# Operand blocks of the feed-forward: other units, a fourth staging tile, and two operands split in the first period

## The chip, the core and the metric

The kernel runs on one core of one Trainium2 chip. The metric is the device time of one execution in microseconds (us), the median of three runs. The core has five engines that work beside each other, each in the order of its own instruction list: PE multiplies matrices, DVE, ACT and POOL work on elements, and SP only issues transfers (ACT issues some too). An instruction that waits holds back everything behind it on its engine. SBUF holds operands, PSUM holds what PE writes, DRAM holds inputs, outputs and what the kernel parks there.

## The reference

One transformer block over 2048 tokens of width 576 in float32, with a conditioning vector `c`:

```python
mod = (_silu(c) @ w_mod).reshape(c.shape[0], 6, 1, -1)
sa, ca, ga, sb, cb, gb = ...                      # six rows of 576
h = _layernorm(x) * (1 + ca) + sa
x = x + ga * attention(h, wq, wk, wv, wo, beta)   # 32 heads of 18, four segments of 512 tokens
h = _layernorm(x) * (1 + cb) + sb
x = x + gb * ((_silu(h @ w_gate) * (h @ w_up)) @ w_down)   # inner width 4608
```

Attention runs inside each segment of 512 tokens under a causal mask and is mixed, by a gate per head, with a linear memory that collects the earlier segments.

## The kernel before

The kernel has three stretches: projections and memory (to about 260 us), attention (to about 632 us), and the feed-forward with the output projection of the last segment at its head.

**Attention** is a loop over 33 units `u` (L1332); a unit is four heads of one segment, so segment `s` is units 8s to 8s+7. A unit has eleven steps `k`. Which small piece of work stands in which step is written out by hand in `PAT`, a table of letters: `M` and `X` are the output projection of an earlier segment, `V` the probabilities times values, `n` the hand-over of row maxima through DRAM (ACT stores them, SP reads them back as `qs<-mD`), and so on. At the start of unit u SP also issues the keys and queries of unit u+3. Besides the table there is a dictionary `sched`, filled by `at(g, f)`, where `g = 11*u + k`: what stands under g is issued at the end of that step.

**The feed-forward** multiplies by seven products instead of eight: tokens come in two halves, features in two halves of 288, and seven combinations of the four blocks (operands 0 to 6 of `y`) meet seven combinations of the weights (`O`). A float32 operand is split into a high part (a cast on ACT) and the rest (a subtraction on DVE); each product is then three products of parts, seven matmuls in all, the last being for the remaining 32 features, held three times over 96 rows. Each block of features is thus three pieces `kb`: 128, 128 and 96 rows.

The operands of the first 1024 tokens are made during attention, by `stage_a` and `stage_b`, which put their work into `sched`:

- `stage_a` takes the first 512 tokens. For six blocks `i` (two feature halves `kh` times three `kb`) it loads the normalized columns from DRAM (`load_cols`, L931, shown as `yh<-xh`), transposes them on PE (`trans4`, `pt`, L947), scales and shifts them on ACT into `yh` (L942), and then, in two column halves, casts (L926), subtracts (L909) and stores the split to DRAM (`yD`, L915 and L917) as operands 0 and 1. The two parts go through a staging tile; three of them are used in turn, one in a free part of `yh` and two in `mbd`, the memory of attention, which is no longer read. Block `i` belongs to unit 18 + i; its transposes stand in the step that `step_of` (table `KP`, L46) gives, its cast two steps later for the first half and five for the second, the subtraction one step after the cast, the store two more.
- `stage_b` takes the other 512 tokens in the same way, block `i` in unit 24 + i. It forms the differences with the first blocks on POOL (L1005) and stores operand 5; the blocks for the others stay in `yh`, nine pieces of 512 columns (`yh[:, k]`, k = 0 to 2).

**The border** begins after the last unit (L1352). SP loads the first weight block `O` (`load_o`, L1114), then operands 0, 1 and 5 (`load_y`, L1103), with the second weight block between operand 0 and 1. POOL forms operand 4 (`y_sum` 0 to 2, L1017) and operand 6 (`y_sum` 3 to 5, L1019) and the sums of the weight blocks (`sum_o`, L1139, four for each block). PE does the output projection of the last segment: 32 pieces `n`, four to a half of 288 columns (`wo_m`, `pw`, L709), into two PSUM banks in turn; after a half DVE adds it to x (`wo_x`, `xr`, L714), which frees the bank. Between the pieces stand, at the numbers in the tables, a weight sum (`SS`, L48), the split of one piece of an operand that stays in SBUF (`HH`, L49, `y_here`, cast L1026, subtractions L1028 and L1030), and the split of weights (`WW`, L47: `prep_w`, `wh` L1148 and `wl` L1149; `prep_r` for the remaining 32 features, `wr` L1133 and L1134). `y_here(j)` is operand 4, 3, 6, 2 for j = 0-2, 3-5, 6-8, 9-11. DVE's part of a split is put on a list and issued after the next piece (`flush`).

**Periods.** Then come 2 x 18 periods `p` of fourteen steps (L1440). A step issues what the step before put on the list, casts the weights needed five products later, and then one product (`step`, `prod`, L1184). In period 0 the products of the first half use operands 0, 4, 1, 5, 3, 6 in steps 0 and 2 to 6 and operand 2 in step 8 (`ZM`, L898; `ACT_OP`, L900). Products collect in the PSUM banks A, B and C; ACT copies partial results out of A (`cu`, `tb`, `tc`, L1213) and DVE finishes others (L1199 to L1208). After the first copy ACT issues the stores of both summed weight blocks (`store_o`, `oD<-O`, L1123, L1486). The next weight block is loaded into the buffer of the first once that is stored and its splits are done. In period 0 POOL also scales and sums the down-projection weights (`dr_`, L1162, L1167). From period 1 on, a generator `prep2` (L1032) makes the operands of the other 1024 tokens a step at a time; its pool `x2p` is opened before period 0.

## Time and profile before

| what | value |
|---|---|
| median of three runs | 1934.17 us (1931.89 to 1936.68) |
| the profiled execution's own time | 1936.01 us |
| its span, first to last instruction | 1934.3 us, at a mean clock of 0.993 |
| PE busy | 1879.5 us, 97% of the span |
| DVE, ACT, POOL busy | 1508.3, 934.0, 578.6 us |
| units 18 to 31 | about 461 to 632 us |
| the border, until the first feed-forward product | about 632 to 663.7 us |

The chain that ended last is followed back from the last instruction, at each step to what released it. A timeline line reads: start, duration, engine, line of the kernel, operation, output and inputs, shapes and count; the square brackets hold the idle time of that engine just before, and what ended it. A window line gives, for a stretch of time, its length and then the busy time of PE, PE's weight loads, DVE, ACT and POOL, with the number of instructions, then the clock that PE was granted, the busy share of the transfer engines and GB/s.

### The profile page before, as it was taken

The numbers are of one execution on the slowest core, as the hardware profiler recorded it, in microseconds if no ns is written. First come the engines' busy times: TensorE is split into PE (matmuls) and PEld (weight loads), VectorE is DVE, ScalarE is ACT, GpSimd is POOL, SyncE is SP. The second block draws the span as 40 slices with busy tenths as digits, with TensorE's granted clock in tenths as the row PEclk, the third lists the DMA queues.
The fourth block names the chain that finished last, engine by engine and source line by source line (L and its number), as shares of the span: only waits on it lengthen the run. The fifth ranks groups of instructions, "written<-read, shape, count | busy, mean of one in ns | idle before, by whom it ended". The sixth has DMA issues, their size and how long they took to land.

```text
span 1934.3 us, 30685 instructions
## 1 busy us (share of the span) xinstructions
PE 1879.5 (97%) x10927; PEld 1564.6 (81%) x10927; DVE 1508.3 (78%) x3270; ACT 934.0 (48%) x2057; POOL 578.6 (30%) x778
## 2 busy tenths in 40 slices
PE   7999999999999799999999999999999999999999
PEld 4888865676666678888888888888888888888888
DVE  6475257878776688888888988876888888888887
ACT  2222256767667444445445444444545444454542
POOL 5222235455455464544553544410000000000000
PEclk9999999999999899999999999999999999999999
DMA  7767565445753755455455454468333233332331
GB/s 214 236 228 247 200 201 142 131 139 161 186 146 102 237 181 199 148 184 176 148 174 170 156 168 154 137 232 280 100 96 107 94 122 101 121 101 92 107 109 61
DMA packets 178409, 304.12 MB, mean 157 GB/s; under 512 B 25648, under 2 KB 105968, under 8 KB 176400
## 3 DMA queue, kind: packets, MB, share of 16 engines
q1 hardware_dynamic: 148144, 244.56, 40.7%
q10 hardware_dynamic: 30112, 57.60, 8.5%
q8 instruction: 86, 1.41, 0.3%
q14 instruction: 67, 0.55, 0.1%
HBM read 189.02 MB, written 113.05 MB: 156 GB/s over the span
## 4 chain that ended last, share of the span: by engine, by line
PE 85%; DMA 6%; DVE 4%; ACT 1%; issue 1%; POOL 1%; SPq 1%; DVEq 0%; POOLq 0%; ACTq 0%
PE A L1184 23%; PE pd L1305 12%; PE C L1184 11%; PE pd L1288 9%; PE B L1184 6%; PE pp L98 4%; PE s L586 4%; PE av L606 3%; PE s L184 3%; PE pv L98 3%; PE pw L709 2%; DMA y<-yD 2%; DMA mD<-mr 1%; PE pn L780 1%; DMA wml<-in_w_mod_dram 1%
## 5 line engine op out<-in xcount | busy, mean ns | idle before, releaser
L1184 PE MATMUL A<-y,wh 128*128 128x512 f32 x1152 | 406.8, 394 | 2.9 <-DMA y<-yD 1.5
L189 DVE CUSTOM_DVE_ANT_0 junk<-s,tri 128x256 bf16<-128x256 f32 (+3 forms) x512 | 228.8, 486 | 79.2 <-PE s L184 70.0
L1149 DVE TENSOR_TENSOR wl<-O,wh 128x256 fp32r<-128x256 f32 x504 | 264.5, 530 | 3.6 <-ACT wh L1148 3.1
L1184 PEld LDWEIGHTS A<-y,wh 128*128 128x128 f32 x1152 | 217.1, 188 | 47.6 <-issue 1.7
L1184 PE MATMUL A<-y,wl 128*128 128x512 f32 x576 | 227.2, 394 | 0.0
L589 ACT ACTIVATE Pt<-s 128x512 f32<-128x512 f32 (+1 forms) x352 | 187.1, 559 | 81.8 <-PE s L586 64.8
L1139 POOL TENSOR_TENSOR O<-O 128x384 f32<-128x384 f32 x144 | 162.3, 1139 | 186.6 <-DMA O<-in_wgu_dram 81.3
L1293 DVE TENSOR_TENSOR acc<-acc,pd 128x576 f32<-128x576 f32 x216 | 162.5, 752 | 58.6 <-PE pd L1288 51.8
L1184 PE MATMUL C<-y,wh 128*128 128x512 f32 x576 | 202.8, 393 | 3.8 <-DVE cu L1207 3.8
L1148 ACT CAST wh<-O 128x256 fp32r<-128x256 f32 x504 | 196.7, 405 | 2.0 <-DVE wr L1134 1.0
L1305 PE MATMUL pd<-dh,ah 128*128 128x288 f32 x640 | 189.2, 296 | 0.1
L1305 PE MATMUL pd<-dh,al 128*128 128x288 f32 x640 | 189.1, 295 | 0.0
L1305 PE MATMUL pd<-dl,ah 128*128 128x288 f32 x640 | 188.9, 295 | 0.0
L1309 DVE TENSOR_TENSOR acc<-acc,pd 128x576 f32<-128x576 f32 x156 | 116.9, 749 | 87.1 <-PE pd L1305 86.9
L1248 ACT CAST ah<-sg 128x512 fp32r<-128x512 f32 x192 | 119.1, 620 | 85.7 <-DVE sg L1208 85.5
L586 PE MATMUL s<-qs,ks 110*128 110x512 f32 (+2 forms) x384 | 150.2, 408 | 8.8 <-DMA qs<-mD 4.3
L184 PE MATMUL s<-ks,qs 108*128 108x256 f32 (+3 forms) x512 | 141.5, 328 | 4.1 <-DVE mx L189 1.9
L1249 DVE TENSOR_TENSOR al<-sg,ah 128x512 fp32r<-128x512 f32 x192 | 136.0, 708 | 9.1 <-ACT ah L1248 8.8
L1288 PE MATMUL pd<-dh,ah 128*128 128x288 f32 x448 | 133.0, 297 | 0.0
L1288 PE MATMUL pd<-dh,al 128*128 128x288 f32 x448 | 132.5, 296 | 0.0
L1288 PE MATMUL pd<-dl,ah 128*128 128x288 f32 x448 | 132.3, 295 | 0.0
L1184 PEld LDWEIGHTS C<-y,wh 128*128 128x128 f32 x576 | 108.3, 188 | 24.4 <-DVE cu L1207 4.2
(353 smaller groups left out, 4413.6 us busy)
## 6 DMA issues: line engine op xcount, KB each, us to landing
O<-in_wgu_dram SPq DMA_DIRECT2D x36, 768.0 KB
oD<-O ACTq DMA_DIRECT2D x36, 512.0 KB
O<-oD SPq DMA_DIRECT2D x36, 512.0 KB
ks<-kD SPq DMA_DIRECT2D x68, 216.0 KB
qs<-qD SPq DMA_DIRECT2D x68, 216.0 KB
O<-in_wgu_dram SPq DMA_DIRECT2D x36, 384.0 KB
rD<-wr ACTq DMA_DIRECT2D x36, 336.0 KB
wr<-rD SPq DMA_DIRECT2D x35, 336.0 KB
```

The costliest lines, as they stand in the source:

```text
L184: nc.tensor.matmul(bank[:, n * (h - h0):n * (h - h0) + n], lhsT=qst[b][0:108, h, 128 * i:128 * i + 128], rhs=kst[b][0:108, h // 2, 0:n], s ...
L189: nc.vector.tensor_tensor_reduce(junk[:, :n], bank[:, n * (h - h0):n * (h - h0) + n], tri[:, L - n:], 1.0, -3e38, op0=ALU.add, op1=ALU.max ...
L586: nc.tensor.matmul(bank[:, n * (g - h):n * (g - h + w)].rearrange("p (a b) -> p a b", a=w), lhsT=kst[u % NB][0:110, g // 2, 128 * j:128 * ...
L589: nc.scalar.activation(pt[:, h:h + per, :n], bank[:, :n * per].rearrange("p (a b) -> p a b", a=per), AF.Exp, scale=SCALE)
L1139: nc.gpsimd.tensor_tensor(o[:, d], o[:, a], o[:, b], op=op)
L1148: nc.scalar.copy(wh, o)
L1149: later.append(lambda: nc.vector.tensor_tensor(wl, o, f32(wh), op=ALU.subtract))
L1184: nc.tensor.matmul(bank, lhsT=a, rhs=b, start=(first and n == 0), stop=(n == 6), skip_group_check=not first)
L1249: later.append(lambda: nc.vector.tensor_tensor(al, src, f32(ah), op=ALU.subtract))
L1288: nc.tensor.matmul(pd[:, i, :288], lhsT=a[:, tk], rhs=w, start=(k == 0), stop=(k == 2))
L1293: nc.vector.tensor_tensor(o, o, pd[:, :, :288], op=ALU.add)
L1305: nc.tensor.matmul(pd[:, i, :288], lhsT=a[:, tk], rhs=w, start=(k == 0), stop=(k == 5))
```

## The change

Five things are changed.

1. `stage_a`: the first block's transposes stand in step 10 of unit 18 instead of step 7, and its casts, subtractions and stores move with them. A fourth staging tile is used in turn with the three, in `gaB`, a row of the conditioning that is not read any more.
2. `stage_b`: block `i` belongs to unit 25 + i instead of 24 + i. Its load stands in step 1 of the unit before, for the first block too.
3. `yh` becomes two tiles: one for k = 0, which lives until the end of the output projection as before, and one for k = 1 and 2, which lives until period 1. There the pool `x2p` is now opened.
4. At the border all six `y_sum` are issued before the first weight sum, and the second weight block is loaded after operands 1 and 5. Four weight sums stand later in the output projection (`SS`).
5. Operands 4 and 3 are split during the output projection, at other pieces (`HH`). The six pieces of operands 6 and 2 are split in steps 0 to 5 of period 0 (`HP`), each just ahead of that step's product in the issue order.

```diff
@@ -45,8 +45,9 @@
 PM = ()
 KP = (7, 8, 1, 3)
 WW = (9, 11, 14, 18, 26)
-SS = (2, 3, 4, 5, 18, 20, 22, 24)
-HH = (4, 6, 8, 10, 12, 13, 15, 17, 19, 21, 23, 25)
+SS = (2, 3, 4, 5, 25, 27, 29, 30)
+HH = (4, 6, 8, 12, 16, 20)
+HP = (0, 1, 2, 3, 4, 5)
 XP = (3, 1, 0, 0, 0, 0)
 LD = 2
 LM = 3
@@ -650,11 +651,16 @@
             vq[s] = vp.tile([P, 4, VC], F32, tag="vq", name=f"vq{s}")
         nc.sync.dma_start(vq[s][:, j, :], vD[s][:, j, :])
 
+    p7 = ExitStack()
+    yh12 = pool(p7, "yx2", side="right").tile([P, 2, 3, L], F32, tag="yh12", name="yh12")
     w3 = pool(p2r, "w3", side="right")
     o3 = pool(p2r, "o3", 2, side="right")
     op = pool(p2r, "op", side="right")
-    yx = pool(p2r, "yx", side="right")
-    yh = yx.tile([P, 3, 3, L], F32, tag="yh", name="yh")
+    yh0 = pool(p2r, "yx", side="right").tile([P, 3, L], F32, tag="yh0", name="yh0")
+
+    def yh(k, kb):
+        return yh12[:, k - 1, kb] if k else yh0[:, kb]
+
     woh = w3.tile([P, 5, D], F32R, tag="woh", name="woh")
     wol = w3.tile([P, 5, D], F32R, tag="wol", name="wol")
 
@@ -953,22 +959,22 @@
         return a.rearrange("p a b -> p (a b)")
 
     def stage_a():
-        sc = flat(yh[:, 2])
+        sc = flat(yh12[:, 1])
         xb = [sc[:, L * i:L * i + L].rearrange("p (a b) -> p a b", b=P) for i in range(2)]
         mb = mbd[:, 0:2].rearrange("p a b c -> p (a b c)")
-        st = [v.rearrange("p (a b) -> p a b", b=256).bitcast(F32R) for v in (sc[:, 2 * L:3 * L], mb[:, :L], mb[:, L:2 * L])]
+        st = [v.rearrange("p (a b) -> p a b", b=256).bitcast(F32R) for v in (sc[:, 2 * L:3 * L], mb[:, :L], mb[:, L:2 * L], gaB[:, :L])]
         pts = {}
         for i in range(6):
             kb, kh = divmod(i, 2)
             u = 18 + i
             n = P if kb < 2 else 96
-            h = yh[:, kh, kb]
+            h = yh(kh, kb)
             at(11 * (u - 1) + 1 if i else 11 * u, lambda i=i, kh=kh, kb=kb: load_cols(xb[i % 2], 0, 0, kh, kb))
-            g = step_of(u)
+            g = step_of(u) if i else 11 * u + 10
             at(g, lambda i=i, n=n: trans4(xb[i % 2], n, pts, i))
             at(g + 1, lambda i=i, h=h, kh=kh, kb=kb: scaled(h, flat(pts.pop(i)), kh, kb))
             for hv in range(2):
-                y_part(g + 2 + 3 * hv, kh, kb, h[:, 256 * hv:256 * hv + 256], lambda j=2 * i + hv: st[j % 3], hv)
+                y_part(g + 2 + 3 * hv, kh, kb, h[:, 256 * hv:256 * hv + 256], lambda j=2 * i + hv: st[j % 4], hv)
 
     def stage_b():
         big = flat(sk2.tile([P, 5, L], F32, tag="pq", name="yq"))
@@ -985,12 +991,12 @@
 
         for i in range(6):
             hv, kb = divmod(i, 3)
-            u = 24 + i
+            u = 25 + i
             n = P if kb < 2 else 96
             c = slice(256 * hv, 256 * hv + 256)
-            h00, h11 = yh[:n, 0, kb, c], yh[:n, 2, kb, c]
+            h00, h11 = yh(0, kb)[:n, c], yh(2, kb)[:n, c]
             a, b = h10[i % 2], t3[i % 2]
-            at(11 * (u - 1) + 1 if i else 11 * u, lambda i=i, hv=hv, kb=kb: load(i, hv, kb))
+            at(11 * (u - 1) + 1, lambda i=i, hv=hv, kb=kb: load(i, hv, kb))
             g = step_of(u)
 
             def trans(i=i, n=n):
@@ -999,7 +1005,7 @@
             def sc(i=i, kb=kb, a=a, c=c):
                 pt = flat(pts.pop(i))
                 scaled(a, pt[:, 0:256], 0, kb)
-                scaled(yh[:, 2, kb, c], pt[:, 256:512], 1, kb)
+                scaled(yh(2, kb)[:, c], pt[:, 256:512], 1, kb)
 
             def sub2(d, x, y_):
                 nc.gpsimd.tensor_tensor(d, x, y_, op=ALU.subtract)
@@ -1012,7 +1018,7 @@
     def y_sum(j):
         q, kb = divmod(j, 3)
         n = P if kb < 2 else 96
-        t1, t4, h11, t2 = [v[:n] for v in (yh[:, 0, kb], yh[:, 1, kb], yh[:, 2, kb], ys[:, kb])]
+        t1, t4, h11, t2 = [v[:n] for v in (yh(0, kb), yh(1, kb), yh(2, kb), ys[:, kb])]
         if q == 0:
             nc.gpsimd.tensor_tensor(t2, h11, t1, op=ALU.subtract)
         else:
@@ -1021,7 +1027,7 @@
     def y_here(j):
         o, kb = (4, 3, 6, 2)[j // 3], j % 3
         n = P if kb < 2 else 96
-        f = ys[:, kb] if o == 4 else yh[:, (3, 6, 2).index(o), kb]
+        f = ys[:, kb] if o == 4 else yh((3, 6, 2).index(o), kb)
         d = y[:, o, kb if kb < 2 else 4]
         nc.scalar.copy(d[:n], f[:n])
         if kb < 2:
@@ -1029,7 +1035,7 @@
         else:
             later.append(lambda: nc.vector.tensor_tensor(d[64:96], f[64:96], f32(d[64:96]), op=ALU.subtract))
 
-    def prep2():
+    def prep2(x2p):
         ha = xp.tile([P, 2, L], F32, tag="xs", name="ha")
         xb = xp.tile([P, 4, 2, P], F32, tag="xs", name="xb")[:, :, 0]
         t3 = x2p.tile([P, 256], F32, tag="t3", name="t3")
@@ -1363,12 +1369,12 @@
         p5 = ExitStack()
         ys = pool(p5, "ys").tile([P, 3, L], F32, tag="ys", name="ys")
         load_o(0, 0, 0)
-        for j in range(3):
+        for j in range(6):
             y_sum(j)
         load_y(0, 0)
-        load_o(0, 0, 1)
         load_y(0, 1)
         load_y(0, 5)
+        load_o(0, 0, 1)
         wo_z(3)
         wo_r(3, 0)
         wo_z2(3)
@@ -1389,8 +1395,6 @@
                     if n in SS:
                         j = SS.index(n)
                         sum_o(0, j // 4, j % 4)
-                    if n in (7, 9, 11):
-                        y_sum(n // 2)
                     if n in HH:
                         y_here(HH.index(n))
                     if n in WW:
@@ -1411,8 +1415,6 @@
         ap_ = pool(p4, "ap", 4)
         ps = pool(p4, "ps4", 1, space=PSUM)
         p6 = ExitStack()
-        x2p = pool(p6, "x2p")
-        g2 = prep2()
         new_acc(accp, (2, 3, 4, 5))
         seq = [(p, z, m) for t in range(2) for p in range(NPR) for z in range(2) for m in MP]
         late = {}
@@ -1429,6 +1431,10 @@
                 dl = 2 if t == 0 and p == 0 else 0
                 nx = (p + 1) % NPR
                 tn = t if nx else t + 1
+                if t == 0 and p == 1:
+                    p7.close()
+                    x2p = pool(p6, "x2p")
+                    g2 = prep2(x2p)
                 if t == 0 and p == NPR - 1:
                     run(g2)
                     p6.close()
@@ -1448,6 +1454,8 @@
                         f()
                     while acts:
                         acts.pop(0)()
+                    if dl and k in HP:
+                        y_here(6 + HP.index(k))
                     if k != 1 or prev is not None:
                         step(z, m)
                     if k == 1 and prev is not None:
```

## The prediction

> **What bounds the kernel now.** I read the page first, then the chain that ended last in order of time, then the timelines of PE, ACT, DVE and POOL around each place where that chain leaves PE.
>
> The page and the chain (start us, us, what):
>
> ```profile
> span 1934.3 us, 30685 instructions
> PE 85%; DMA 6%; DVE 4%; ACT 1%; issue 1%; POOL 1%; SPq 1%; DVEq 0%; POOLq 0%; ACTq 0%
> 461.36 7.84 DMA yh<-xh
> ...
> 488.92 8.72 DMA yD<-mbd
> ...
> 541.49 6.78 DMA yq<-xh
> ...
> 641.05 14.56 DMA y<-yD
> ```
>
> PE holds 85% of the chain; three transfers of the operand blocks and one stretch at 641 us stand in it. The chain's length is not the price: a landing hides behind PE until PE runs dry. The price is PE's idle time before the instruction that waited, in square brackets in PE's timeline:
>
> ```profile
> 469.24 0.66 PE L947 MATMUL pt<-ident,yh 128*128 128x128 f32 x4 [0.67 <-DMA yh<-xh]
> 498.56 0.50 PE L586 MATMUL s<-qs,ks 110*128 110x512 f32 x1 [1.82 <-ACT Pt L589]
> 551.78 0.63 PE L666 MATMUL ptr<-ident,o 128*64 128x128 f32 x4 [1.12 <-ACT yh L942]
> 655.76 0.61 PE L709 MATMUL pw<-woh,oh 128*128 128x288 f32 x1 [6.47 <-DVE xr L714]
> 692.71 0.50 PE L1184 MATMUL C<-y,wh 128*128 128x512 f32 x1 [3.77 <-DVE cu L1207]
> ```
>
> The causes, in ACT's, DVE's and POOL's timelines:
>
> ```profile
> 497.72 0.40 ACT L926 CAST mbd<-yh 128x256 fp32r<-128x256 f32 x1 [2.65 <-DMA yD<-mbd]
> 649.63 1.09 DVE L1134 TENSOR_TENSOR wr<-O,wr 32x512 fp32r<-32x512 f32 x1 [1.56 <-ACT wr L1133]
> 652.06 1.75 DVE L1028 TENSOR_TENSOR y<-yh,y 128x512 fp32r<-128x512 f32 x1
> 653.85 1.37 DVE L1030 TENSOR_TENSOR y<-yh,y 32x512 fp32r<-32x512 f32 x1
> 655.24 0.46 DVE L714 TENSOR_TENSOR xr<-pw,xr 128x288 f32<-128x288 f32 x1
> 644.10 4.85 POOL L1139 TENSOR_TENSOR O<-O 128x384 f32<-128x384 f32 x4 [6.82 <-DMA O<-in_wgu_dram]
> 648.90 4.36 POOL L1019 TENSOR_TENSOR yh<-yh,ys 128x512 f32<-128x512 f32 x3
> 676.37 2.10 POOL L1139 TENSOR_TENSOR O<-O 128x384 f32<-128x384 f32 x2 [17.74 <-DVE wl L1149]
> ```
>
> At 497.72 ACT waits for a staging tile still being stored, and the exponentials that PE needs stand behind it. From 649.63 DVE works without a gap; xr, which empties the product bank that PE wants next, is fifth in that queue. The last two windows are the clock after two of these waits (columns: PE, PEld, DVE, ACT, POOL busy, then PEclk):
>
> ```profile
> 499.00:503.00 4.00, 4.00 (x22) 2.65 (x21) 2.86 (x16) 1.84 (x4) 3.24 (x7) 0.57 0.96 299
> 656.00:660.00 4.00, 3.79 (x16) 3.47 (x17) 3.97 (x7) 0.09 (x1) 2.64 (x3) 0.54 0.26 99
> ```
>
> **Part 1, blocks of units 18 to 23.** Nothing is added: the same 12 casts, subtractions and stores. The first block's transposes move three steps later (7 to 10 of unit 18). Unit 18 to 24 take 80 us, 13.3 a unit, 1.2 a step, so they come at about 473, after the landing at 469.2: the 0.67 goes. With four tiles, a tile's next cast comes at least ten steps (12 us) after its store is due, where the shortest distance was four. The cast at 497.72 becomes the sixth; its tile's store now goes out at about 486, ahead of the next unit's key and query loads (before, 488.92 behind them), and has nine us to land. So the 2.65 on ACT goes, and PE's 1.82. The four us after it ran at clock 0.57, which lost 4.00 x 0.43 = 1.7. On SP the first block's two stores go behind the 0.25 us issue of qs<-mD; that issue came at 484.10, and the first of them is wanted again at 491.20, which the store issued at 484.44 already met. Sum: -0.67 - 1.82 - 1.7 = -4.2.
>
> **Part 2, units 25 to 30.** The first load stays in unit 24 (one step later) and its transposes come a unit later, 18 steps after it: the landing at 548.3 is covered and the 1.12 goes. Elsewhere the blocks use steps that blocks already used, except unit 30. There the last load (six transfers, whose issue took 6.18 us at 589.56) starts in unit 29, at about 600.5, after the xD store, and PE wants it eleven steps on, near 612. Issue to 606.7 and a tail like that of the chain's small loads, about 2, give 608.7: hidden with three us to spare; without that cover it costs 0 to 3. It also pushes the next qs<-mD on SP from 605.17 to about 606.7; that lands by 609 and unit 30 wants it near 611. Sum -1.1.
>
> Late next in both parts: DVE, busy 11.82 of 14 us in 474 to 488, and the 0.61 idle at 486.04 behind a cast of the same kind, which the change leaves. Of the 5.3 I give back 0.8 (ends: 0, and the 3.4 that would leave only the staging wait): -4.5.
>
> **Part 3, sums and loads at the border.** POOL's three second sums (4.36 us) move to 637.3, into the 6.82 us in which it waited for O: free, ended by 642. On SP the second weight load moves behind two operand loads; all are in one queue that moves about 330 GB/s until 656, so it lands near 655.6. Its four POOL sums (1.0 to 1.35 each) end by 660.5. ACT's store of that block is queued behind cu in period 0, at about 662: covered by 1.5 us; without cover each us late holds ACT and then PE.
>
> **Part 4, fewer splits ahead of xr.** Before 649.63 nothing moves: xr of the third half waits for the first O as before. After it DVE has wr, wl, one y, xr. POOL is now idle there (its next data come at 655.6), so I take the uncontended rows: wr 0.68, wl 0.41, y 0.69. xr starts at 649.63 + 1.78 = 651.4, not 655.24: -3.8. The gap shrinks from 6.47 to 2.6. Contention as before would give 649.63 + 1.09 + 1.39 + 1.75 = 653.9, -1.4: the low end. The clock: a 1.82 gap was followed by half clock, so I expect one such window here (before, 3.73 us busy at 0.50 in 652.9 to 659.6, 1.9 lost; one window loses 1.7): -0.2. If the clock stays up, -1.9. The next halves wait for xr with at most one y ahead of each: nothing. Sum -4.0 (ends -1.4 and -5.7): the feed-forward starts near 659.7, not 663.72.
>
> **Part 5, two operands in period 0.** Six casts, 0.52 from start to start, 3.1 us of ACT; six subtractions at 0.61, 3.7 us of DVE. DVE's gaps between 664.7 and 680.4 are 2.56, 1.71, 1.30, 0.31, 1.61 and 1.70, 9.2 in all. ACT is tight: two casts stand before tb, one before each of the next, and the copy tc, which frees the bank for the seventh product, ends 1.0 late for PE. PE catches up: it waits 0.47 for tb, 0.23 for tc and 3.77 at 692.71 anyway, and those come from POOL's sums at 676.37, which start when O lands after the oD store, all of it tied to cu and not to the casts. The operands are ready two steps before use. I charge +0.3 (ends 0, and 14.2 if all is in the open at the contended 1.75 and 0.62). The pool opened a period later holds nothing that runs before period 1: 0; what would cover it otherwise is PE's 35 us period.
>
> Sum: -4.5 - 4.0 + 0.3 = -8.2. Against the profiled execution's 1936.0 this is 1927.8; that execution stands 1.8 above the median of the three runs, so on the median 1934.17 - 8.2 = 1926.
>
> **A rule weighed.** Part 4 stands on y, wr and wl being slow at 649 to 655 because POOL ran. Rows: y takes 0.68 with POOL idle and up to 1.75 beside it, while xr, one of whose inputs is in PSUM, took 0.45 beside POOL's sums at 646.59. By these rows the step is -3.8; if the long durations had another cause it is -1.4 and the sum -5.6. The Trainium skill, "SBUF — State Buffer", Who interferes with whom, has a lock held for a whole instruction when a DVE instruction with two SBUF inputs meets a POOL instruction that reads SBUF; by that the sum is -8.2, and the rows agree. The same rule speaks against Part 3, whose early sums would lock the y splits at 640.14 and 642.01. Worked out from rows, that is up to 1.07 each, 2.1; DVE has 0.41 to spare before it waits for O, so xr at 646.59 comes up to 1.7 later, and PE, which then waits that much less at 651, gets it back.
>
> **The rivals.** (a) The clock does not halve after the shorter gap at 651. Price -1.7: 1924; with Part 1 and 2 in full, 1923.5. For it: the 1.00 gap at 647 was followed by clock 1.00. Against: the 1.82 gap was not. The Trainium skill, "TensorE: Matmul & The Clock Gate", Part 1, puts the drop after an idle window of about 3.4 us, which would make this rival the forecast; the row at 499 disagrees, since 1.82 sufficed. (b) Only one place pays: DVE takes over the attention waits (-4.0 + 0.3, 1930.5), or contention keeps Part 4 at its low end (-4.5 - 1.4 + 0.3, 1928.6). DVE's 11.82 of 14 speaks for the first. (c) The edit does not do it: the second O lands so late that ACT's store holds period 0 back by what was won; needs the landing eight us later than 655.6, against a queue whose bytes are the same. 1934. (d) Slower: the moved splits run in the open. If period 0 has no room, because tc's lateness pushes DVE's subtractions past POOL's start at 676.37, they cost 14.2 and a half-clock window 1.7, less 8.5 won: 1941.5. It decides once more than DVE's 9.2 us are used up; 3.7 are asked.
>
> **How the numbers follow.** About 0.3% (5.8 us) is what a measurement can tell from no change: 1928.4 and 1940.0. Forecast 0.55, its own range 1923 to 1930; (a) 0.13; (b) 0.16; (c) 0.07; (d) 0.09. Faster: 0.50 of the forecast, all of (a), 0.03 of (b), 0.66. Slower: (d), 0.09. Same: the rest, 0.25. The range leaves out (d) and the outer parts of (a) and (c): 1920 to 1934.
>
> **What would show it.** No wait of ACT for a yD store near 497 and clock 1.00 after it; no PE gap at the first transposes of units 18 and 24; PE's gap before the fourth half near 2.5 with xr at 651 to 652; first product near 659 minus the 4.5 won before; POOL idle from 649 to the second O; six y casts among period 0's with the 3.77 wait still there. It is wrong if a new PE wait in period 0 exceeds 2 us, or if the attention units take as long as before.

## The result

The changed kernel takes 1924.0 us (median; 1922.0 to 1929.4), the kernel before in the runs beside it 1931.9 (1927.9 to 1936.7). The ratio is 0.9961 with a 95% interval of 0.9949 to 0.9973: 7.5 us faster, 5.2 to 9.8. Repeated beside the runs of other kernels it was 0.9959 (0.9946 to 0.9972). The forecast was 8.2 us faster. The sum came out; the terms did not, and they missed in opposite directions, so that the sum fits is luck.

The profiled execution took 1929.36 us, the longest of the eleven. Line numbers up to about L650 are one higher than before, those behind six higher. The page's first line and the shares of the chain that ended last:

```profile
span 1927.6 us, 30678 instructions
PE 88%; DMA 5%; DVE 3%; ACT 2%; issue 1%; POOL 1%; SPq 1%; ACTq 0%; DVEq 0%; POOLq 0%
```

The chain in order of time (start, duration, what), around the units of the operand blocks:

```profile
466.03 5.20 DMA mD<-mr
471.29 1.85 DMA qs<-mD
...
478.58 6.04 DMA mD<-mr
484.64 2.09 DMA qs<-mD
...
505.44 7.40 DMA mD<-mr
512.86 2.05 DMA qs<-mD
```

The three transfers of operand blocks have left the chain. In their place stands the hand-over of the row maxima, ACT's store and SP's read-back, which the experiments call the hop. PE's timeline, the lines with waits that answer to those of before:

```profile
473.28 0.47 PE L587 MATMUL s<-qs,ks 110*128 110x512 f32 x1 [0.27 <-DMA qs<-mD]
486.87 0.77 PE L587 MATMUL s<-qs,ks 110*128 110x512 f32 x1 [1.95 <-DMA qs<-mD]
645.67 0.37 PE L715 MATMUL pw<-woh,oh 128*128 128x288 f32 x1 [2.48 <-DVE xr L720]
649.83 0.61 PE L715 MATMUL pw<-woh,oh 128*128 128x288 f32 x1 [1.56 <-DVE xr L720]
668.39 0.50 PE L1190 MATMUL A<-y,wh 128*128 128x512 f32 x1 [0.99 <-ACT tc L1219]
688.11 0.79 PE L1190 MATMUL C<-y,wh 128*128 128x512 f32 x1 [3.95 <-DVE cu L1213]
```

The waits at 469, 498 and 551 are gone, and one of 1.95 for the read-back is there. The gap before the fourth half is 1.56, not 6.47. DVE's, POOL's and ACT's timelines at the border and in period 0:

```profile
647.67 0.68 DVE L1140 TENSOR_TENSOR wr<-O,wr 32x512 fp32r<-32x512 f32 x1 [2.14 <-ACT wr L1139]
648.38 0.43 DVE L1155 TENSOR_TENSOR wl<-O,wh 128x256 fp32r<-128x256 f32 x1
648.73 0.69 DVE L1034 TENSOR_TENSOR y<-yh,y 128x512 fp32r<-128x512 f32 x1
649.33 0.45 DVE L720 TENSOR_TENSOR xr<-pw,xr 128x288 f32<-128x288 f32 x1
...
656.36 4.66 POOL L1145 TENSOR_TENSOR O<-O 128x384 f32<-128x384 f32 x4 [9.37 <-DMA O<-in_wgu_dram]
669.73 2.79 POOL L1145 TENSOR_TENSOR O<-O 128x384 f32<-128x384 f32 x2 [8.71 <-DMA O<-in_wgu_dram]
661.61 0.41 ACT L1154 CAST wh<-O 128x256 fp32r<-128x256 f32 x1 [1.95 <-POOL O L1145]
670.26 1.39 DVE L1140 TENSOR_TENSOR wr<-O,wr 32x512 fp32r<-32x512 f32 x1
671.68 3.86 DVE L1155 TENSOR_TENSOR wl<-O,wh 128x256 fp32r<-128x256 f32 x3
```

The windows behind the new wait (the clock is the third number from the end):

```profile
486.00:490.00 4.00, 3.13 (x13) 1.53 (x14) 1.65 (x5) 1.19 (x2) 1.71 (x4) 0.57 0.94 299
490.00:494.00 4.00, 4.00 (x22) 2.77 (x23) 1.10 (x3) 2.12 (x5) 0.00 (x0) 0.57 0.90 210
```

In front of xr DVE has the four steps that were forecast, at the short durations that were forecast. ACT waits 1.95 for the second weight block, which the forecast had covered. In period 0 the subtractions wr and wl stand beside POOL's sums and take 1.39 and 1.29 each. After the wait at 487 PE ran at half clock for 6.8 us.

**Where the time went, stretch by stretch.** One profile of each kernel would mislead here, so every experiment below was also read as a further execution of the parts that it leaves alone. For the same matmul in two traces, its start in one minus its start in the first trace of before is the lead or lag at that place; the difference between two places is what the stretch won (negative) or lost. In us, with places on the clock of before's first profile:

| trace | attention 445-625 | border 625-662 | period 0, 662-720 | first product to end of the wait for cu |
|---|---|---|---|---|
| before, first profile | 0 | 0 | 0 | 29.0 |
| before, second profile | -2.3 | +0.8 | +1.2 | 29.2 |
| attention parts alone | -4.5 | +0.2 | +1.4 | 29.6 |
| border parts alone | -1.8 | -7.3 | +3.7 | 30.7 |
| changed, first profile | -1.8 | -4.9 | +1.7 | 30.8 |
| changed, second profile | -3.6 | -7.9 | +3.8 | 30.7 |
| second store later | -4.3 | -5.4 | +1.5 | 30.6 |
| block loads behind the hop | -2.5 | -5.2 | +1.5 | 29.9 |
| no block loads, units 20 to 23 | -6.0 | -5.1 | +0.7 | 29.6 |
| load order as before | -4.7 | -3.3 | +1.2 | 30.2 |
| all splits at the border | -3.3 | -2.9 | +0.9 | 28.7 |
| Part 3 undone | -5.2 | -2.8 | +1.9 | 30.3 |
| cu first | -2.9 | -6.7 | +1.5 | 27.8 |
| stores behind B | -4.2 | -7.0 | -0.5 | 26.6 |

The 445 us ahead, the same code everywhere, came between 5.7 us earlier and 1.1 us later than in before's first profile: that much a difference of two single profiles means nothing. Likewise about 1.7 us near 1316, where before's first profile has a wait of 1.50 for an operand, are gone in its second too, while the run with Part 3 undone has 1.2 of that wait again: chance, not the change.

Old attention code: 0, -2.3, -1.8, mean -1.4. New, nine traces (without the two that change the block loads): mean -3.8. So Parts 1 and 2 won about **2.4**, not 4.5; the three old values spread over 2.3 us and the nine new ones over 3.4, so the figure is rough. Border and period 0 together: old 0, +2.0, +1.6 (mean 1.2); changed -3.2 and -4.1, border parts alone -3.6 (mean -3.6): **4.8** won, where 3.7 was forecast. Sum 7.2, against 7.5 by the times.

### The profile page after: what moved, and what is told of

It reads as the page before. It is cut to its first block, busy times and chain, and to the rows that moved or that the text cites. A ratio compares the mean times of both kernels' runs of the same rounds, so it can differ in the third digit from the quotient of the medians.

```text
span 1927.6 us, 30678 instructions
## 1 busy us (share of the span) xinstructions
PE 1882.8 (98%) x10927; PEld 1568.8 (81%) x10927; DVE 1506.7 (78%) x3270; ACT 933.9 (48%) x2057; POOL 579.2 (30%) x778
## 4 chain that ended last, share of the span: by engine, by line
PE 88%; DMA 5%; DVE 3%; ACT 2%; issue 1%; POOL 1%; SPq 1%; ACTq 0%; DVEq 0%; POOLq 0%
PE A L1190 23%; PE pd L1311 13%; PE C L1190 12%; PE pd L1294 9%; PE B L1190 6%; PE pp L99 5%; PE s L587 4%; PE av L607 4%; PE s L185 4%; PE pv L99 3%; PE pw L715 2%; DMA mD<-mr 2%; DMA O<-in_wgu_dram 1%; PE pn L786 1%; PE px L628 1%
```

## The experiments

**Attention parts alone** (before, with Parts 1 and 2):

```diff
-        ... mb[:, :L], mb[:, L:2 * L])]
+        ... mb[:, :L], mb[:, L:2 * L], gaB[:, :L])]
-            g = step_of(u)
+            g = step_of(u) if i else 11 * u + 10
-  ... st[j % 3]
+  ... st[j % 4]
-            u = 24 + i
+            u = 25 + i
-            at(11 * (u - 1) + 1 if i else 11 * u, ... load(i, hv, kb))
+            at(11 * (u - 1) + 1, ... load(i, hv, kb))
```

> The kernel before with Parts 1 and 2 alone (blocks moved, fourth tile), border and period 0 untouched. Theory T: the row maxima that pass through DRAM (store by ACT, read back by SP) come next late, because their hop takes 5 to 7 us while a block load is in the queue and 1.4 us when it is not; so PE waits 0.2 to 2 us for qs<-mD in units 19 to 21, and the border is reached only 1.5 to 2.5 us earlier: ratio to before near 0.999. Rival P (as predicted): the 1.95 us wait at 486.87 is a chance of that one execution, and the attention units give 4.5 us: ratio 0.9977.

Measured: 0.9996 (0.9987 to 1.0005), 0.8 us faster, between 2.5 faster and 1.0 slower. PE's waits in the attention stretch are now all of one kind:

```profile
483.79 0.47 PE L586 MATMUL s<-qs,ks 110*128 110x512 f32 x1 [1.00 <-DMA qs<-mD]
497.52 0.47 PE L586 MATMUL s<-qs,ks 110*128 110x512 f32 x1 [0.42 <-DMA qs<-mD]
510.85 0.47 PE L586 MATMUL s<-qs,ks 110*128 110x512 f32 x1 [0.96 <-DMA qs<-mD]
```

The three waits of the operand blocks are gone; 2.38 us at the read-back remain. The interval leaves out rival P's 0.9977 and holds theory T's 0.999.

**Border parts alone** (changed, with `stage_a` and `stage_b` as before):

```diff
-        ... mb[:, L:2 * L], gaB[:, :L])]
+        ... mb[:, L:2 * L])]
-            g = step_of(u) if i else 11 * u + 10
+            g = step_of(u)
-            u = 25 + i
+            u = 24 + i
...
```

> The changed kernel with the blocks of units 18 to 23 and 24 to 29 as before (three tiles), border and period 0 changed. Theory T: the waits at 469, 498 and 551 us are back; from border to first product 4.9 us are won, period 0 gives back 1.7; ratio 0.998 to 0.9985. Rival P: 4.0 won and 0.3 given back, 0.998: the time does not tell these apart, the profile does (ACT waits 1.5 to 2 us for POOL's sums behind the second store of period 0 under T, under 0.5 under P).

Measured: 0.9986 (0.9974 to 0.9997), 2.7 us faster, 0.6 to 5.0. The three waits at the operand blocks are back (0.89, 1.30 and 1.13), the border is 7.3 shorter and period 0 takes 3.7 back. ACT stands still for 2.57 us behind the second store, which goes out as POOL's sums end (656.54): T's sign, not P's. The times of this run and the one before add up to 3.5 where both changes together gave 7.5. Their intervals reach 2.5 and 5.0, and the stretches give 2.4 and 4.8, so nothing forces an interaction; that there is none isn't shown.

**The second store later.** ACT's 1.95 wait at 661.6 is for the sums of the second weight block, whose store stands in step 0 of period 0. Here the store stands in step 3:

```diff
                         if k == 0 and p == 0:
                             store_o(p, 0)
-                            store_o(p, 1)
                         elif k == 3:
+                            if p == 0:
+                                store_o(p, 1)
                             store_r(p, 0)
```

> The changed kernel; the store of the second summed weight block moves from step 0 to step 3 of period 0. Theory S: the 1.7 us that period 0 gives back is the wait of ACT for POOL's sums in front of that store (1.95 us); without it the gap from first product to the C product of period 1 shrinks from 30.7 to about 29 us and the time falls 1.5 us below the changed kernel. Rival C: it is the six casts and subtractions; the gap stays at 30.5 us or more, and the time with it.

Measured: 0.9959 (0.9945 to 0.9974), and 30.6 us from the first product to the end of the wait for cu against 30.8. ACT no longer waits there, and it brings nothing that can be told: the store's wait was not what period 0 gave back.

**Block loads behind the hop.** If the block loads ahead of the read-back on the queue make it late, loads a unit earlier, issued behind it, should help:

```diff
-  xb = [sc[:, L * i:L * i + L]... for i in range(2)]
+  xb = [v... for v in (sc[:, :L], sc[:, L:2 * L], yh(1, 2))]
-  at(11 * (u - 1) + 1 if i else 11 * u, ... load_cols(xb[i % 2], 0, 0, kh, kb))
+  at(11 * (u - 2) + 5 if i > 1 else 11 * 18 + i, ... load_cols(xb[i % 3], 0, 0, kh, kb))
...
-  at(11 * (u - 1) + 1, ... load(i, hv, kb))
+  at(max(11 * (u - 2) + 5, 11 * 24 + 1), ... load(i, hv, kb))
```

> The changed kernel; the block loads stand one unit earlier, right behind the read-back of the row maxima, in a third load buffer (a piece of yh not yet written; for the second stage a free part of yq). Theory T: the hop takes 1.4 to 3 us in units 18 to 29 instead of 3 to 7, no wait of PE for qs<-mD above 0.3 us is left there, and the border comes 3 to 4 us earlier than in the changed kernel: ratio to before near 0.994. Rival P: the hop is not what PE waits for in most executions, and the time stays that of the changed kernel, 0.996.

Measured: 0.9968 (0.9956 to 0.9979), no gain. Three waits at the read-back stayed, 0.73, 0.66 and 1.50 (at 484, 498 and 512). From the issue of the store to the issue of the read-back it took 4.7 and 5.0 us in the first two of these units; behind that 5.9, 3.5 and 1.8. The last wait ended 7.4 us after its read-back was issued at 504.3, with three block loads issued right behind it; that these held it up is inferred.

**No block loads in units 20 to 23:**

```diff
+            if i < 2:
                 at(11 * (u - 1) + 1 if i else 11 * u, ... load_cols(xb[i % 2], 0, 0, kh, kb))
```

> The changed kernel without the loads of the third to sixth operand block of units 20 to 23 (their transposes use the first two blocks' data again, so the operands that come of it are others). Theory T: the waits at qs<-mD in units 20 to 23 (1.95 at 487, 0.24 at 515) are due to the block loads that share the queue with the read-back of the row maxima. Then from the issue of the store of the maxima to the issue of the read-back it takes 1.4 to 3 us in units 20 to 23 and not 3.8 to 7.4, no wait at qs<-mD is over 0.2 us there, and the stretch from 485 to 530 is about 2 us shorter. Rival: the key, query and value loads of the next units and the stores fill the queue by themselves; then the hop still takes 4 to 6 us and the waits stay, each 0.3 to 1.5.

Measured, in a single execution of 1920.7 us: one wait of 1.01 at 481.8 is left instead of 1.0 to 1.95 and up to two more of up to 1.0, and the attention stretch is 6.0 shorter, the most of all. But the hop still took 5.2, 4.3 and 6.4 us for the stores at 474.5, 487.9 and 497.9. So the block loads may make up part of the waits (1.0 in all here, 1.6 to 2.4 in the nine traces with the new code), which one execution doesn't show, and neither theory is right by itself: the hop is long without them too. It is also long in units that never had a block load: 5.69 us for the store at 284.49 and 5.73 for that at 318.45, in the first profile of before. What else makes it long (the key, query and value loads in flight, or other stores) wasn't taken away and stays open.

**The kernel before, again.**

> The kernel before, unchanged, profiled in a second execution. The prediction read three waits of the operand blocks (0.67 at 469, 1.82 at 498, 1.12 at 551) and the half clock behind the second as fixed properties of the kernel. If they are, this execution shows the same three within 0.3 us each, the stretch from 445 to 625 takes the same time within 1 us, and the time is the same as the kernel before's. Rival (chance): the waits depend on how transfers happen to meet in one execution; then at least one of the three is gone or has another size by over 0.7 us, the stretch differs by 1.5 us or more, and the 1.50 us wait for y<-yD near 1316, which only the kernel before's first profile had, is absent.

Measured: 1.0010 (0.9993 to 1.0027). PE's waits:

```profile
469.26 0.66 PE L947 MATMUL pt<-ident,yh 128*128 128x128 f32 x4 [0.41 <-DMA yh<-xh]
486.41 0.47 PE L586 MATMUL s<-qs,ks 110*128 110x512 f32 x1 [1.48 <-DMA qs<-mD]
498.37 0.50 PE L586 MATMUL s<-qs,ks 110*128 110x512 f32 x1 [1.25 <-ACT Pt L589]
549.70 0.63 PE L666 MATMUL ptr<-ident,o 128*64 128x128 f32 x4 [1.13 <-ACT yh L942]
645.14 0.37 PE L709 MATMUL pw<-woh,oh 128*128 128x288 f32 x1 [2.48 <-DVE xr L714]
653.71 0.61 PE L709 MATMUL pw<-woh,oh 128*128 128x288 f32 x1 [5.79 <-DVE xr L714]
```

The three waits are properties of the kernel, but two of them vary (0.67 and 0.41; 1.82 and 1.25), and no half clock follows them here. The wait of 1.48 for the read-back is in the *old* kernel too. In the first profile it did not show: there PE waited 0.61 at that place, put down to a cast on ACT. The third half's gap of 1.00, too, was the odd one; it is 2.48 here.

**Load order as before** (Part 3 in part):

```diff
         load_y(0, 0)
+        load_o(0, 0, 1)
         load_y(0, 1)
         load_y(0, 5)
-        load_o(0, 0, 1)
```

> The changed kernel with the second weight block loaded between the first and second operand again, as before. Part 3 priced the order of the loads at nothing. By the steps of the prediction the second block's sums on POOL then run from about 648 to 653, beside the subtractions in front of the third half's xr, so those take 1.09, 1.39 and up to 1.75 and not 0.68, 0.43 and 0.69: PE's wait for xr grows from 1.56 to about 4, the first product comes 2.4 later; against it ACT's 1.95 wait in front of the second store of oD goes and the splits at 658 to 660 (0.88 and 1.49 beside POOL) run in 0.43 and 0.69: 0 to 1 us back. Sum: 1.5 to 2.5 us slower than the changed kernel. Rival: the order matters less than the moved splits; then the first product comes within 0.7 us of the changed kernel's and the time is 1 us shorter.

Measured: 0.9966 (0.9954 to 0.9977). The gap before the fourth half is 2.42, not 4, the rows ahead of xr 0.68, 1.12 and 1.48. Border and period 0 together are 2.1 ahead of before's first profile and so 3.3 ahead of the old mean, where the changed kernel is 4.8 ahead: 1.5 worse, the low end of what was expected. The times can't tell that.

**All twelve splits at the border, the sums still ahead** (Parts 4 and 5 undone):

```diff
-HH = (4, 6, 8, 12, 16, 20)
-HP = (0, 1, 2, 3, 4, 5)
+HH = (4, 6, 8, 10, 12, 13, 15, 17, 19, 21, 23, 25)
+HP = ()
```

> The changed kernel with all twelve splits at the border again, the sums still in front. Undoes Part 4 and Part 5 together. By the prediction: PE's wait for xr before the fourth half goes from 1.56 back to about 6, the border is 3.8 to 5 longer, and period 0 wins 0.3 back: 3.7 us slower than the changed kernel. Rival C (the six casts and subtractions push DVE's wr and wl beside POOL's sums of the next weight block, and that is what period 0 gave back): from the first product to the end of the wait for cu period 0 takes 29.0 as in the kernel before and not 30.8, so the net is 2.2 to 3.2 slower.

Measured: 1922.7, 0.9956 (0.9933 to 0.9979): by the times not slower than the changed kernel. The gap did not go back to 6. DVE's and PE's timelines:

```profile
640.68 0.68 DVE L1140 TENSOR_TENSOR wr<-O,wr 32x512 fp32r<-32x512 f32 x1 [1.55 <-ACT wr L1139]
641.39 0.42 DVE L1155 TENSOR_TENSOR wl<-O,wh 128x256 fp32r<-128x256 f32 x1
641.73 0.68 DVE L1034 TENSOR_TENSOR y<-yh,y 128x512 fp32r<-128x512 f32 x1
642.45 0.68 DVE L1036 TENSOR_TENSOR y<-yh,y 32x512 fp32r<-32x512 f32 x1
643.16 0.46 DVE L720 TENSOR_TENSOR xr<-pw,xr 128x288 f32<-128x288 f32 x1
...
643.68 0.61 PE L715 MATMUL pw<-woh,oh 128*128 128x288 f32 x1 [2.32 <-DVE xr L720]
```

xr is fifth in the queue as before, and yet early, because POOL is idle (its sums ended at 640.0 and start again at 648.9): four steps take 2.5 us instead of 5.6. In period 0 the same splits, absent, let DVE do wr and wl ahead of POOL's sums, which start 12.3 us after the first product in this run and 12.4 in the changed kernel:

```profile
662.16 0.68 DVE L1140 TENSOR_TENSOR wr<-O,wr 32x512 fp32r<-32x512 f32 x1
662.87 0.43 DVE L1155 TENSOR_TENSOR wl<-O,wh 128x256 fp32r<-128x256 f32 x1
663.57 0.76 DVE L1155 TENSOR_TENSOR wl<-O,wh 128x256 fp32r<-128x256 f32 x2 [0.28 <-ACT wh L1154]
...
664.06 2.23 POOL L1145 TENSOR_TENSOR O<-O 128x384 f32<-128x384 f32 x2 [10.14 <-DMA acc<-xD]
```

1.87 us for what takes 5.25 in the changed kernel, and period 0 reaches the end of the wait for cu after 28.7 us, not 30.8. Rival C is right on where period 0 gave back. Border and period 0 together are 2.0 ahead of before's first profile, where the changed kernel is 3.2 and 4.1 ahead: by the stretches, this kernel is some 1.6 us behind it.

**Splits alone** (changed, with Part 3 undone):

```diff
-SS = (2, 3, 4, 5, 25, 27, 29, 30)
+SS = (2, 3, 4, 5, 18, 20, 22, 24)
-        for j in range(6):
+        for j in range(3):
             y_sum(j)
...
+                    if n in (7, 9, 11):
+                        y_sum(n // 2)
```

> The changed kernel with Part 3 undone (the three second sums and the second weight block's load and sums where they were), Parts 1, 2, 4 and 5 kept: six splits fewer at the border, POOL busy beside the rest as before. If the number of splits ahead of xr was the price, as the name of Part 4 has it, PE's gap before the fourth half is 2.5 to 3.5 as in the changed kernel and the border keeps its 4 to 6. Theory D (what made them late was POOL beside them, and Part 3 moved POOL away; seven splits more or fewer hardly count, as the run with all twelve at the border had a gap of 2.32): the rows in front of xr stay at 1.1, 1.4 and 1.75, the gap is 4.0 to 5, and the border keeps only 1.5 to 2.5 of what was won. The prediction's own low end for Part 4 (contention as before) was -1.4.

Measured: 0.9982 (0.9972 to 0.9991). DVE ahead of xr, beside POOL, and PE's gap:

```profile
642.47 1.09 DVE L1140 TENSOR_TENSOR wr<-O,wr 32x512 fp32r<-32x512 f32 x1 [2.14 <-ACT wr L1139]
643.59 1.38 DVE L1155 TENSOR_TENSOR wl<-O,wh 128x256 fp32r<-128x256 f32 x1
644.90 1.75 DVE L1034 TENSOR_TENSOR y<-yh,y 128x512 fp32r<-128x512 f32 x1
646.57 0.45 DVE L720 TENSOR_TENSOR xr<-pw,xr 128x288 f32<-128x288 f32 x1
...
647.07 0.61 PE L715 MATMUL pw<-woh,oh 128*128 128x288 f32 x1 [4.51 <-DVE xr L720]
```

Theory D: six splits fewer leave the durations at 1.1, 1.4 and 1.75 and the gap at 4.5. From a mean of 5.9 in the three old traces, POOL's sums alone (the run with all twelve splits) bring the gap to 2.3, the moved splits alone to 4.5, and both together, in the changed kernel and in the border parts alone, to 0.9 to 1.6. In the gap POOL's sums are worth more. Over the whole border the two runs are level, 2.9 and 2.8 ahead of before's first profile, where Theory D expected less of this one; but the run with all twelve splits has 10.2 us at half clock there and this one 6.8. With period 0 they are 3.2 and 2.1 ahead of the old mean, of the 4.8 for both. Each is one trace, and the intervals of the times overlap, so beyond the gap the ranking isn't shown.

**The changed kernel, again.**

> The changed kernel, unchanged, in a second execution. The waits at qs<-mD (1.95 at 487 in its first profile) should come again with 1.0 to 2.0, as in the four runs that share its attention part; the stretch from 445 to 625 should be 2.5 to 4.7 shorter than in the first profile of the kernel before (the first profile of the changed kernel, with 1.8, is then the odd one), the border 5 to 6 shorter, and the time 1924 within 1.5.

Measured: 1924.14, 0.9959 (0.9946 to 0.9972); the read-back's waits are 1.60 and 0.33. The border was 7.9 shorter, 3.0 more than in the first profile: its two gaps before xr are 0.8 shorter together, and no half clock fell on it, where the first profile has 6.8 us. Period 0 gave back 3.8.

**cu first.** The second store stands later, as above, and in step 12 of period 0 the sum that empties bank C goes ahead of the subtractions:

```diff
+                    cu1 = dl and k == 12
+                    if cu1:
+                        step(z, m)
                     for f in todo:
                         f()
...
-                    if k != 1 or prev is not None:
+                    if not cu1 and (k != 1 or prev is not None):
                         step(z, m)
```

> The changed kernel with the second store of oD three steps later and, in step 12 of the first period, the sums that empty bank C (cu, sg) ahead of the subtractions wl, dl and al on DVE. In the changed kernel PE waits 3.95 at 688 for cu, which could start at 684.2, when C is complete, and starts at 687.4 behind wl, dl and al beside POOL's sums (1.21 + 1.24 + 1.27). If DVE's order is what this wait is made of, it shrinks to 0.7 to 1.5, and 2.5 to 3.2 us go; the half clock that follows it may go too (1.7 more): 1919 to 1921, the wait not found again elsewhere in the period. Rival: PE then waits for the subtraction that was pushed back (wl of the next period, or al), or for POOL's sums that all of it hangs on; then the period takes the same 30.5 and the time is that of the changed kernel.

Measured: 1921.7, 0.9946 (0.9932 to 0.9961). The wait for cu fell to 0.99, and the next place took over, as the rival has it:

```profile
678.08 0.50 PE L1190 MATMUL C<-y,wh 128*128 128x512 f32 x1 [0.99 <-DVE cu L1213]
682.51 0.50 PE L1190 MATMUL A<-y,wh 128*128 128x512 f32 x1 [2.54 <-ACT B L1236]
...
679.73 0.52 ACTq L1129 DMA_DIRECT2D oD<-O  x1
680.67 0.34 ACTq L1509 DMA_DIRECT2D wd<-dr__8794  x1
681.05 0.62 ACT L1254 CAST ah<-sg 128x512 fp32r<-128x512 f32 x1 [5.79 <-DVE dl L1180]
681.88 0.58 ACT L1236 COPY B<-A 128x512 f32<-128x512 f32 x1
```

The last four lines are ACT's: the copy into B stands behind two stores. They go out as POOL's sums end (679.71 and 680.64), 0.02 and 0.03 later, so the wait belongs to POOL, though the row ahead of the copy names DVE. Period 0 as a whole takes as long as with the later store alone (+1.5 in the table), and the interval of the time overlaps with that of the changed kernel: moving cu by itself can't be told from nothing.

**Stores behind B.** The same, for step 13 too, with the two stores behind the copy:

```diff
-                    cu1 = dl and k == 12
+                    cu1 = dl and k >= 12
...
-                        elif k == 13 and tn == 0:
+                        elif k == 13 and tn == 0 and p:
                             store_o(nx, 1)
-                        if k == 12 + dl // 2:
+                        if k == 0 and p == 1:
+                            store_o(1, 1)
+                            nc.scalar.dma_start(wdD[0][:, :NS[0]], RW[0][:, :NS[0]])
+                        if k == 12 and not dl:
```

> The run with cu first, and besides: ACT's last store of oD and its store of wd of the first period issued behind the copy into bank B and not in front of it, and step 13's sum (sg from A) also ahead of DVE's subtractions. In the run with cu first PE's wait for cu went from 3.95 to 0.99, but 2.54 came at 682.5 for the copy into B, which stood on ACT behind these two stores, and they behind POOL's sums (ended 679.7 and 680.6). If the end of period 0 hangs on ACT's queue and so on POOL, this wait shrinks to 0.3 to 1.0, the stretch 662 to 720 is 1.5 to 2.2 shorter than there, and the time is 1919 to 1920.5. Rival: PE is held at the next place by POOL all the same (the subtractions wl and al beside its sums, or the later store delays the load of dr): the stretch is within 0.7 of the run with cu first and the time 1921 to 1923.

Measured: 1921.3, 0.9934 (0.9919 to 0.9950): 12.8 us faster than the kernel before, 9.7 to 15.7. Period 0 takes 2.0 us less than in the run before this, as expected, but the time doesn't show it: 1921.3 lies where the rival had it (1921 to 1923), 0.5 below the run before. PE's waits at the two places are down to:

```profile
680.23 0.50 PE L1190 MATMUL C<-y,wh 128*128 128x512 f32 x1 [0.29 <-DVE cu L1213]
683.24 0.50 PE L1190 MATMUL A<-y,wh 128*128 128x512 f32 x1 [1.12 <-ACT B L1236]
```

Of what is left, 1.88 at 688.6 for the copy tb comes behind them. The interval just touches that of the changed kernel and does not hold its ratio: by about 5 us the faster of the two. How much of that belongs to the last edit alone can't be told from the times.

## Why the prediction was right, and where it was not

- **The sum** (-8.2) lies inside the measured -5.2 to -9.8, by terms of -4.5, -4.0 and +0.3 that measured about -2.4, -7 and +2.2 by the stretches (for the last two, means of the changed kernel's two traces and the border alone, against three old ones). The errors, +2.1, -3.0 and +1.9, nearly cancel. Nothing in the prediction makes them do so: that is luck.
- **Part 1, "so the 2.65 on ACT goes, and PE's 1.82".** They went: no trace with the new code has a wait for a staging tile. The step that failed is "late next in both parts: DVE". Late next was the read-back of the row maxima, 1.0 to 1.95 in the unit at about 485 and up to 1.0 in later ones. It was late in the old kernel already (1.48 in its second profile, 1.44 with the border parts alone), where the staging wait twelve us later stood beside it. The waits account for what was won: the three that the prediction named come to 3.2 on the mean of the three old traces and are gone, and the waits at the read-back grew from 1.2 to 2.1, so 2.3 are left. The 0.8 given back was about right in size, for another reason than the one given.
- **Part 1, "lost 4.00 x 0.43 = 1.7".** The term was a single execution's. Neither other trace of the old code has half clock in this stretch, while four of nine with the new code do (3.4 us three times, 6.8 once). This term, 1.7 of the 2.1 by which Parts 1 and 2 together fell short, is the one that was mis-sized.
- **Part 2, -1.1.** Held: 1.12 or 1.13 in all three old traces, no such wait in the new ones. The last load in unit 30 was hidden, as forecast.
- **Part 3, "covered by 1.5 us".** The cover was the difference of two forecast times, 662 for ACT and 660.5 for the end of the sums, and both moved. With each trace's own lead at the start of the border taken out, ACT came at 660.6, 657.6 and 658.3 in the changed kernel's two traces and the border alone, because the border got 4.9 to 7.9 us shorter and not 4.0; the sums ended at 662.5, 660.1 and 660.8. So ACT waited 1.95, 2.42 and 2.57. The term of 0 was right all the same: moving the store won nothing. The contention that the rule weighed against Part 3 came: beside POOL's early sums the y splits took 1.73 and 1.40 (after, 637.14 and 639.16), not 0.68. It didn't show in PE's wait before the third half, 1.80 to 2.48 against 1.00 to 2.48 in the old traces. And Part 3 was more than free. Without it the gap before the fourth half is 4.5.
- **Part 4, -3.8 for xr and -0.2 for the clock.** The mechanism held step by step: four steps at 0.68, 0.43, 0.69 and 0.45. The two gaps before xr together fell from 7.5, 8.3 and 7.5 in the old traces to 4.0, 3.2 and 2.7, by 4.4 on the means (forecast 3.9). The clock term was mis-sized. Old traces have 10.2, 13.7 and 13.7 us at half clock at the border, the changed kernel 6.8 and 0, the border alone 3.4. The prediction weighed only the piece at 652.8; it passed over the one at 635.8 in the same trace, which stands behind gaps of 1.07 and 0.95. Half of such time is lost where PE is busy in it: at most 4.5 on the means; what the border won beyond the gaps is 7.0 - 4.4 = 2.6, not 0.2. Its name, "fewer splits", is only part of it: all twelve at the border, with the sums ahead, still give a gap of 2.3. The Trainium skill, "SBUF — State Buffer", Who interferes with whom, states the contention of DVE instructions with two SBUF inputs and POOL's reads; the rows agree (y 0.68 with POOL idle, 1.75 beside it).
- **Part 5, +0.3.** Measured +1.6: 30.7 from the first product to the end of the wait for cu, against 29.1 on the mean of the four traces without splits there. The step that failed: the waits "come from POOL's sums at 676.37, which start when O lands after the oD store, all of it tied to cu and not to the casts". (The row shown for 676.37 names DVE's wl as what ended POOL's wait; in the first profile of the changed kernel it is the landing of O.) The casts and subtractions push wr and wl past POOL's start, where they take 5.25 instead of 1.87. That is rival (d)'s mechanism, small: it was to decide once DVE's 9.2 us of gaps are used up, but the gaps were not all ahead of POOL's start. The other 0.6 of period 0's 2.2 stays open. Half clock doesn't account for it on the means: two of the three new traces have 6.8 us there and one 3.4, and so have the three old ones.
- **The rivals.** (a) fell in the first trace: 6.8 us at half clock, from 647.0, so already behind the third half's gap of 2.48 and not behind the one at 651. In the second trace the clock stayed up, so no forecast from the gap alone could settle it. (b) came in part: the read-back, and not DVE, took over 0.9 of the attention waits. (c) had its wait, 1.95 and more on ACT, without its price.

## What to carry to other kernels

A wait read in one profile is a price only if a second execution of the same kernel shows it with the same size; the second profile of before has 2.8 us of the 5.3 from which the attention term was made. When a queue of short DVE instructions is late, look first at what POOL runs beside it: here, moving POOL's work out of the way shortened PE's wait by 3.6, and taking DVE's work away by 1.4. And a store that is "covered" by 1.5 us is covered only as long as the stretch ahead of it doesn't win more than was forecast: here it won 0.9 to 3.9 more.

## What was unexpected in the hardware

- Half clock comes in pieces of 3.41 us (3.4, 6.8, 10.2 and 13.7 in these traces) and does not follow from the length of PE's gap. In attention it followed gaps of 1.82, 1.95, 1.60, 1.75, 1.67 and 1.50, and did not follow 1.66, 1.85, 1.48, 1.44, 1.37 or anything shorter. Where the border begins, every trace has the same two gaps, 1.07 and 0.95, two us apart; in two of fourteen traces half clock stands behind them (before at 635.8, cu first at 629.3). The Trainium skill, "TensorE: Matmul & The Clock Gate", Part 1, puts the drop after an idle window of about 3.4 us and calls the window free-running: the length of the pieces agrees, while a gap of about half a window was enough, sometimes.
- A store of 16 KB followed by its read-back takes 1.4 us from issue to issue in some units (before, 362.50 to 363.90) and 7.4 in others, with 2 more until the read-back lands. It is among the smallest transfers of the kernel, where most move 100 KB and more, and it is the one that PE waited for.
- The same 445 us of code, in fourteen executions, differ by up to 6.8 us.
